# An adaLN transformer block on one core: a prologue with on-chip block table, uniform folds, split state banks and paired modulation groups

## The chip, the cores and the metric

The kernel runs on one NeuronCore of a Trainium2 chip. The metric is the time of one execution on the device in microseconds. A kernel is run several times and the median is given. One more execution is recorded by the hardware profiler; it has a time of its own, and its span is the time from its first to its last instruction.

The engines are named as the profile names them: PE (TensorE, matrix products, with PEld for its weight loads), DVE (VectorE), ACT (ScalarE), POOL (GpSimd) and SP (SyncE, which here only issues DMAs).

## What is computed

```python
x = A_x                                         # 2048 x 640
mod = (silu(c) @ w_mod).reshape(1, 6, 1, 640)
sa, ca, ga, sb, cb, gb = (mod[:, i] for i in range(6))
h = layernorm(x) * (1 + ca) + sa
q, k, v = split(h @ wqkv)                       # 32 heads of 20
pq, pk = q @ w_phi, k @ w_phi                   # per head, 20 x 20
phi = lambda p: concat(softmax(p), softmax(-p))
kv = phi(pk)^T v;  z = sum over s of phi(pk)    # per head
o = (phi(pq) kv) / (phi(pq) z + 1e-6)
x = x + ga * (o @ wo)
h = layernorm(x) * (1 + cb) + sb
out = x + gb * (relu(h @ w1 + b1)^2 @ w2 + b2)  # inner width 1728
```

All data are 32-bit floats. Large products are made of three products of a high and a low part of each operand (`three`, line 84).

## The kernel before

The 2048 tokens are 16 tiles of 128. The work has a **prologue** (lines 146 to 638), a **planned part** in which a planner orders the instructions of the token tiles 2 to 13 (lines 650 to 687), and later parts for the output projection and the two MLP products, whose order is again written out by hand. This case is about the prologue; there the order on every engine is that of the program, once `manual_schedule` is entered (line 196).

The prologue loads weights, folds `w_phi` into the weights of Q and K, computes the scale and shift of the first layer norm for 640 features as columns, and runs the projections of the tiles 0 and 1.

- **Loads.** SP's queue issues them in this order (lines 198 to 232): `c`, the block table `bd`, K's weights (`wk1`, the last 40 columns, then five blocks of 128 rows), x's tokens 0 to 255 (`load_x(0)`), Q's weights in the same way, modulation blocks 0 and 1 (`load_wm`), x's tokens 256 to 511, modulation blocks 2 to 4, V's weights.
- **Block table.** `bd_t` has 128 rows and 640 columns: for a group of six heads a block of 120 x 120, with each head's 20 x 20 matrix on its diagonal, five such groups, and two heads in the last 40 columns. The host fills it, with zeros around the diagonal, and the kernel loads it whole (lines 199 and 200).
- **Warm-up.** `WARM` = 14 products of a tile of ones (line 563) keep PE working until the first weights are there.
- **Folds.** `fold(nm, d)` (line 246) makes 128 rows of a folded weight from six products, five with 120 rows of contraction and one with 40 (`GR`, line 26). Each goes to two banks of PSUM from the pool `pj`, which has four banks. The function that it returns, `split`, copies them to SBUF as a high part (ACT) and subtracts it for the low part (DVE).
- **State.** `kvp` (line 143) is one PSUM tile of three banks. From the first key tile on it collects phi(K)^T V in banks 0 and 1; before that its halves (`half`, `TR`) hold the transposes of the normalised tokens (`t_in`) and the columns of the modulation.
- **Modulation.** For each of five groups of 128 features `mod_rows2(d)` multiplies silu(c) with the block `WM[d]` (10 products), `mod_sb(d)` copies the result to SBUF on ACT, `mod_cols2(d)` transposes it and adds up on DVE; `out0(d)` then applies it to the transposed tokens (ACT twice, DVE once), and `k_step(d)` adds this group's share to the K product of both tiles.
- **Layer norm.** `stats` runs on DVE, with four small operations on POOL; `scale` applies the result on ACT, for 256 tokens at a time.

The order of the last steps (lines 564 to 601): folds k0 to k2, `stats` of x's first block, folds k3 and k4, its `scale`, folds q0 and q1, transposes 0 and 1, fold q2, modulation rows 0, fold q3, columns 0, fold q4, modulation rows 1, transposes 2 to 4, then for each d: columns and `out0` of group d + 1, rows of group d + 2, `k_step(d)`; `stats` of x's second block after step 1 and its `scale` after step 2. After that PK is copied out, and the products Q and V of the tiles 0 and 1 follow (lines 610 to 637).

Of the kernel before, what the change touches and what calls it, by code (L numbers as in the profile page):

```python
# [15 lines left out]
P = 128  # L16
# [18 lines left out]
WARM = 14  # L35
# [16 lines left out]
def kernel(  # L52
# [90 lines left out]
    kvp = psK.tile([P, 3, 512], F32, name="kvp")  # L143


    ones = const.tile([P, P], F32, name="ones")
    nc.gpsimd.memset(ones, 1.0)
    ident = const.tile([P, P], F32, name="ident")
# [45 lines left out]
    ET_ = mybir.EngineType  # L194
    first = tc.manual_schedule(engines={ET_.PE, ET_.DVE, ET_.Activation, ET_.Pool, ET_.SP})
    first.__enter__()

    nc.sync.dma_start(c_t, c)
    bd_t = row("s4", "bd_t")
    nc.sync.dma_start(bd_t, bd)  # L200
    raw, WM, RV, XB = {}, {}, {}, {}

    def load_raw(nm, w5, w1):
        raw[nm] = [tok2("w", f"raw_{nm}{i}") for i in range(3)]
        nc.sync.dma_start(raw[nm][2][:40, 1], w1)
        for d in range(NC):
            nc.sync.dma_start(raw[nm][d // 2][:, d % 2], w5[d * P : (d + 1) * P])

# [14 lines left out]
    for d in range(2):  # L223
        load_wm(d)
    load_x(1)
    for d in range(2, NC):
        load_wm(d)
    for d in range(NC):
        if d % 2 == 0:
            both = tok2("w", f"rawv{d}")  # L230
        RV[d] = both[:, d % 2]
        nc.sync.dma_start(RV[d], wv[d * P : (d + 1) * P])

# [12 lines left out]
    def fold(nm, d):  # L246
# [3 lines left out]
        p = pj(f"fold{nm}{d}")  # L250
        for g, (o, n) in enumerate(GR):
            if g < 5:
                r = raw[nm][d // 2][:n, d % 2, g * P : (g + 1) * P]
            else:
                r = raw[nm][2][:n, 1, d * P : (d + 1) * P]
            nc.tensor.matmul(
                p[g // 3][:, (g % 3) * 120 : (g % 3) * 120 + n], r, bd_t[:n, g * 120 : g * 120 + n],
# [158 lines left out]
    def do_kv(t):  # L416
        v, e = vt[t % 2], EK[t]
        for u, (o, n) in enumerate(UN):
# [3 lines left out]
                kvp[64 * c : 64 * c + 64, g // 4, a : a + 2 * n].rearrange("p (s n) -> p s n", s=2),  # L422
# [92 lines left out]
    def half(b, h):  # L515
        return kvp[:, b, 256 * h : 256 * h + 256]
# [3 lines left out]
    def mod_rows2(d):  # L520

        MR[d] = tp(f"mrow{d}")
        for k in range(NC):
            for s in range(2):
                c = 2 * (k % 2) + s
                a = 256 * k + P * s
                nc.tensor.matmul(
                    MR[d][32 * c : 32 * c + 32, :P], cs[:, k : k + 1].to_broadcast([P, 32]), WM[d][:, a : a + P],
                    start=(k < 2), stop=(k >= NC - 2), skip_group_check=True,
                )  # L530

    def mod_sb(d):
        t = MR[d, "sb"] = row("s1", f"msb{d}")[:, :P]
        nc.scalar.activation(t, MR[d][:, :P], AF.Identity, bias=plus[:, 0:1])

    def mod_cols2(d):
        p = half(0, 1)[:, P * (d % 2) : P * (d % 2) + P]
        nc.tensor.transpose(p, MR[d, "sb"], ident)
        nc.vector.tensor_reduce(
            cols_a.rearrange("p (s d) -> p s d", s=2)[:, :, d],  # L540
            p.rearrange("p (h s r) -> p s h r", h=2, s=2)[:, :, :, 0], axis=AX.X, op=ALU.add,
        )
# [21 lines left out]
    for d in range(3):  # L564
        fold("k", d)()
    n0 = stats(XB[0], "a0")
    for d in range(3, NC):
        fold("k", d)()
    scale(XB[0], *n0)
    for d in range(2):  # L570
        fold("q", d)()
    t_in(XB[0], 0, TR[0])
    t_in(XB[0], 1, TR[1])
    fold("q", 2)()
    mod_rows2(0)
# [989 lines left out]
```

## Time and profile before

| | us |
|---|---|
| median of 3 runs | 801.46 |
| lowest and highest run | 798.03, 801.79 |
| profiled execution | 800.36 |
| its span | 798.7 |
| PE busy in the span | 785.4 |
| PE busy from 7 to 27 us | 19.81 of 20 |
| first fold's first weight load | 6.19 |
| DMA engines busy from 7 to 27 us | 1.02 of 1 |

Times in the trace count from the span's start. Line numbers with an L are those of this kernel. A product in 32 bits shows as two records of PE (14 warm-up products, 28 records). A busy PE is not PE at its peak, since products are pipelined and their ends are modelled. The row of an engine or of DMA activity is busy time, not waiting time; idle time stands in brackets behind a row with what ended it. "PEclk" is the granted clock of TensorE, 1.00 at full speed.

### The profile page before, as it was taken

The numbers are of one execution on the slowest core, as the hardware profiler recorded it, in microseconds if no ns is written. First come the engines' busy times: TensorE is split into PE (matmuls) and PEld (weight loads), VectorE is DVE, ScalarE is ACT, GpSimd is POOL, SyncE is SP. The second block draws the span as 40 slices with busy tenths as digits, with TensorE's granted clock in tenths as the row PEclk, the third lists the DMA queues.
The fourth block names the chain that finished last, engine by engine and source line by source line (L and its number), as shares of the span: only waits on it lengthen the run. The fifth ranks groups of instructions, "written<-read, shape, count | busy, mean of one in ns | idle before, by whom it ended". The sixth has DMA issues, their size and how long they took to land.

```text
span 798.7 us, 15281 instructions
## 1 busy us (share of the span) xinstructions
PE 785.4 (98%) x5983; PEld 750.5 (94%) x5983; DVE 579.3 (73%) x1046; ACT 443.3 (56%) x988; POOL 128.3 (16%) x259
## 2 busy tenths in 40 slices
PE   9999999999999999999999999998999999999997
PEld 8899999999999878898899999998999999999997
DVE  4499889998788688993546666775757667675756
ACT  4667675576753355565777737555364645536431
POOL 3001021010000114331000000131131313213110
PEclk9999999999999999999999999999999999999999
DMA  9713326423120243321347355996575967667450
GB/s 341 279 35 128 115 83 203 148 85 116 67 100 1 82 167 132 116 83 67 116 144 239 130 180 213 284 317 207 160 237 154 278 170 234 200 175 218 122 168 34
DMA packets 50560, 126.30 MB, mean 158 GB/s; under 512 B 5872, under 2 KB 6640, under 8 KB 50488
## 3 DMA queue, kind: packets, MB, share of 16 engines
q1 hardware_dynamic: 33432, 84.32, 31.0%
q0 software_dynamic: 14752, 35.76, 16.3%
q10 hardware_dynamic: 2304, 5.24, 1.7%
q8 instruction: 47, 0.77, 0.4%
q14 instruction: 25, 0.20, 0.1%
HBM read 95.32 MB, written 29.88 MB: 157 GB/s over the span
## 4 chain that ended last, share of the span: by engine, by line
PE 75%; DVE 10%; ACT 6%; issue 4%; POOL 3%; DMA 2%; POOLq 0%; ACTq 0%; DVEq 0%
PE up L78 18%; PE acc L78 14%; PE pk L78 8%; PE pq L78 7%; PE pv L78 7%; PE pwo L78 7%; PE acc3x L78 4%; PE kvp L421 2%; DVE dn L790 2%; DVE scr L788 2%; PE te L829 2%; DMA ring_b<-td_b 1%; PE ta L340 1%; PE tb L340 1%; DVE ezb L809 1%
## 5 line engine op out<-in xcount | busy, mean ns | idle before, releaser
L78 PE MATMUL up<-h,w 128*128 128x256 f32 x1640 | 208.7, 279 | 0.4 <-ACT ft L1149 0.4
L78 PEld LDWEIGHTS up<-h,w 128*128 128x128 f32 x1640 | 197.9, 189 | 1.1 <-ACT ft L1149 0.8
L1149 ACT ACTIVATE ft<-up,b_t 128x256 f32<-128x256 f32 x104 | 49.0, 472 | 106.6 <-PE up L78 106.1
L78 PE MATMUL acc<-w,ra 128*128 128x384 f32 x452 | 100.4, 338 | 0.4
L78 PE MATMUL pwo<-wo,ot 128*128 128x256 f32 (+3 forms) x512 | 83.2, 315 | 0.1
L1150 DVE TENSOR_TENSOR ft<-ft 128x256 f32<-128x256 f32 x104 | 44.0, 423 | 50.5 <-ACT ft L1149 48.8
L78 PE MATMUL pk<-wk,hT 128*128 128x384 f32 (+1 forms) x480 | 77.1, 312 | 0.9 <-ACT hT L352 0.9
L78 PEld LDWEIGHTS pwo<-wo,ot 128*128 128x128 f32 (+1 forms) x512 | 75.7, 188 | 1.9 <-ACT ot L866 0.4
L78 PEld LDWEIGHTS acc<-w,ra 128*128 128x128 f32 x452 | 72.7, 188 | 3.7 <-DVE ra L88 2.0
L78 PE MATMUL pq<-wq,hT 128*128 128x384 f32 (+1 forms) x480 | 74.9, 311 | 0.4 <-ACT k L397 0.4
L78 PE MATMUL pv<-wv,hT 128*128 128x384 f32 (+1 forms) x480 | 75.2, 309 | 0.0
L78 PEld LDWEIGHTS pk<-wk,hT 128*128 128x128 f32 x480 | 71.6, 188 | 2.7 <-ACT hT L352 1.1
L78 PEld LDWEIGHTS pq<-wq,hT 128*128 128x128 f32 x480 | 70.5, 188 | 1.5 <-ACT k L397 0.9
L78 PEld LDWEIGHTS pv<-wv,hT 128*128 128x128 f32 x480 | 70.5, 188 | 0.4
L88 DVE TENSOR_TENSOR ra<-ft,ra 128x384 fp32r<-128x384 f32 (+2 forms) x86 | 36.8, 449 | 34.3 <-ACT ra L1173 21.0
L88 DVE TENSOR_TENSOR h<-hfb,h 128x256 fp32r<-128x256 f32 x40 | 17.0, 425 | 46.4 <-ACT h L352 46.3
L1173 ACT ACTIVATE ra<-ft 128x384 fp32r<-128x384 f32 x48 | 25.2, 526 | 32.6 <-DVE ft L1150 25.2
L78 PE MATMUL acc3x<-w,ra 128*128 128x256 f32 x248 | 43.0, 281 | 0.0
L78 PEld LDWEIGHTS acc3x<-w,ra 128*128 128x128 f32 x248 | 39.5, 188 | 1.6 <-DVE y L1314 1.4
L1259 POOL DMA_DIRECT2D ring_a<-td_a x34 | 18.3, 540 | 129.9 <-PE acc L78 103.3
L792 POOL TENSOR_TENSOR dn<-dn,rs_q 128x64 f32<-128x64 f32 x16 | 14.0, 877 | 128.0 <-DVE dn L790 128.0
L1164 DVE TENSOR_TENSOR ft<-ft 128x128 f32<-128x128 f32 x136 | 33.3, 286 | 1.2
(241 smaller groups left out, 1424.5 us busy)
## 6 DMA issues: line engine op xcount, KB each, us to landing
ring_c<-td_c POOLq DMA_DIRECT2D x34, 384.0 KB, 4.6
ring_a<-td_a POOLq DMA_DIRECT2D x34, 384.0 KB, 4.2
ring_b<-td_b POOLq DMA_DIRECT2D x34, 256.0 KB, 4.5
esp<-eq SPq DMA_DIRECT2D x12, 640.0 KB, 3.0
el<-esp SPq DMA_DIRECT2D x12, 640.0 KB, 3.9
rw<-in_w SPq DMA_DIRECT2D x23, 320.0 KB, 3.1
wm<-in_w_mod SPq DMA_DIRECT2D x20, 320.0 KB, 3.8
xb<-in_x SPq DMA_DIRECT2D x8, 640.0 KB, 4.2
```

Source lines behind the costliest of these rows:

```text
L78: nc.tensor.matmul(o, a, b, start=first and i == 0, stop=last and i == len(terms) - 1, skip_group_check=skip,)
L88: (eng or nc.vector).tensor_tensor(out_lo, full, hi.bitcast(F32), op=ALU.subtract)
L340: nc.tensor.transpose(p[:, i * P : (i + 1) * P], xn[:, i, d * P : (d + 1) * P], ident)
L421: nc.tensor.matmul(kvp[64 * c : 64 * c + 64, g // 4, a : a + 2 * n].rearrange("p (s n) -> p s n", s=2), v[:, u], e[:, :, o : o + n], start ...
L788: nc.vector.tensor_tensor(z, flat(ET[t]), flat(zb), op=ALU.mult)
L790: nc.vector.tensor_reduce(dn.rearrange("p s h -> p (s h)"), heads(z), axis=AX.X, op=ALU.add)
L829: nc.tensor.transpose(p[:m, a : a + P], EU[2 * j + i][:, b : b + m], ident)
L1149: nc.scalar.activation(r, p, AF.Relu, bias=b1_t[:, f : f + 1])
L1150: nc.vector.tensor_tensor(r, r, r, op=ALU.mult)
L1164: nc.vector.tensor_tensor(t[:, o], t[:, a], t[:, b], op=op)
L1173: nc.scalar.activation(a[:, 0, :3], t[:, :3], AF.Copy)
L1259: nc.gpsimd.dma_start(RING[j, n, r], TD[n][r].bitcast(F32R))
```

## The change

- The host gives the 32 matrices of `w_phi` as a 120 x 120 array. The kernel loads that into a corner of `bdc` and spreads it with two products on DVE: the array, repeated, times `own`, a pattern of 120 x 6 ones that POOL makes with one memset and two selections.
- This load and that of `c` are issued by ACT instead of SP.
- `manual_schedule` is entered earlier, before the constants, so POOL's constants are made in the program's order.
- The sixth product of each fold reads 120 rows like the others; the added rows of the weights are zeros that DVE sets with two memsets of 128 x 640 before the loads of `wk1` and `wq1`. Those loads stand behind the first block of their weight.
- All five modulation blocks are loaded ahead of x's second block.
- `kvp` becomes three tiles of one bank. The folds q0 and q3 write to banks 1 and 2 instead of `pj`.
- Modulation groups go in pairs: rows 0 and 1 together, then 2, then 3 and 4, each pair in one bank. The step order is new (below): rows 0 and 1 stand behind fold q3, transposes 1 to 4 behind fold q4, and `scale` of x's second block stands after step 3, behind the last `out0`.
- `WARM` is 9.

The diff, cut to its core:

```diff
-WARM = 14
+WARM = 9
...
     psK_s = ExitStack()
     psK = psK_s.enter_context(tc.tile_pool(name="psK", bufs=1, space=PS))
-    kvp = psK.tile([P, 3, 512], F32, name="kvp")
-
+    kvp = [psK.tile([P, 512], F32, name=f"kvp{b}") for b in range(3)]
+
+
+    ET_ = mybir.EngineType
+    first = tc.manual_schedule(engines={ET_.PE, ET_.DVE, ET_.Activation, ET_.Pool, ET_.SP})
+    first.__enter__()
     ones = const.tile([P, P], F32, name="ones")
     nc.gpsimd.memset(ones, 1.0)
+
+    bdc = row("s3", "bdc")
+    own = bdc[:120, P : P + 6]
+    nc.gpsimd.memset(own, 1.0)
+    nc.gpsimd.affine_select(out=own, in_=own, compare_op=ALU.is_ge, fill=0.0, base=0,
+                            pattern=[[-DH, 6]], channel_multiplier=1)
+    nc.gpsimd.affine_select(out=own, in_=own, compare_op=ALU.is_ge, fill=0.0, base=DH - 1,
+                            pattern=[[DH, 6]], channel_multiplier=-1)
     ident = const.tile([P, P], F32, name="ident")
     make_identity(nc, ident)
     neg = const.tile([P, P], F32R, name="neg")
...
     nc.gpsimd.tensor_tensor(mask5, mask5, mtmp[:80, :40], op=ALU.add)
-    ET_ = mybir.EngineType
-    first = tc.manual_schedule(engines={ET_.PE, ET_.DVE, ET_.Activation, ET_.Pool, ET_.SP})
-    first.__enter__()
-
-    nc.sync.dma_start(c_t, c)
+    nc.scalar.dma_start(bdc[:120, :120], bd)
+    nc.scalar.dma_start(c_t, c)
     bd_t = row("s4", "bd_t")
-    nc.sync.dma_start(bd_t, bd)
     raw, WM, RV, XB = {}, {}, {}, {}
     def load_raw(nm, w5, w1):
         raw[nm] = [tok2("w", f"raw_{nm}{i}") for i in range(3)]
-        nc.sync.dma_start(raw[nm][2][:40, 1], w1)
+        nc.vector.memset(raw[nm][2][:, 1], 0.0)
         for d in range(NC):
             nc.sync.dma_start(raw[nm][d // 2][:, d % 2], w5[d * P : (d + 1) * P])
+            if d == 0:
+                nc.sync.dma_start(raw[nm][2][:40, 1], w1)
     def load_x(j):
         XB[j] = tok2(f"x{j % 2}", f"xb{j}")
...
     load_raw("k", wk5, wk1)
     load_x(0)
     load_raw("q", wq5, wq1)
-    for d in range(2):
+    for d in range(NC):
         load_wm(d)
     load_x(1)
-    for d in range(2, NC):
-        load_wm(d)
     for d in range(NC):
         if d % 2 == 0:
             both = tok2("w", f"rawv{d}")
         RV[d] = both[:, d % 2]
         nc.sync.dma_start(RV[d], wv[d * P : (d + 1) * P])
+
+    by_head = bdc[:120, :120].rearrange("p (g f) -> p g f", f=DH)
+    nc.vector.tensor_tensor(
+        bd_t[:120, :600].rearrange("p (g i f) -> p g i f", i=6, f=DH),
+        by_head[:, :5, None, :].to_broadcast([120, 5, 6, DH]),
+        own[:, None, :, None].to_broadcast([120, 5, 6, DH]), op=ALU.mult
+    )
+    nc.vector.tensor_tensor(
+        bd_t[:120, 600:].rearrange("p (i f) -> p i f", f=DH),
+        by_head[:, 5:6, :].to_broadcast([120, 2, DH]), over(own[:, :2]), op=ALU.mult
+    )
     cs = const.tile([P, NC], F32, name="cs")
     ce = const.tile([P, NC], F32, name="ce")
...
     W = {}
-    def fold(nm, d):
+    def fold(nm, d, p=None):
         w = wslot(f"w{nm}{d}")
         W[nm, d] = w
-        p = pj(f"fold{nm}{d}")
+        p = p or pj(f"fold{nm}{d}")
         for g, (o, n) in enumerate(GR):
             if g < 5:
-                r = raw[nm][d // 2][:n, d % 2, g * P : (g + 1) * P]
+                r = raw[nm][d // 2][:120, d % 2, g * P : (g + 1) * P]
             else:
-                r = raw[nm][2][:n, 1, d * P : (d + 1) * P]
+                r = raw[nm][2][:120, 1, d * P : (d + 1) * P]
             nc.tensor.matmul(
-                p[g // 3][:, (g % 3) * 120 : (g % 3) * 120 + n], r, bd_t[:n, g * 120 : g * 120 + n],
+                p[g // 3][:, (g % 3) * 120 : (g % 3) * 120 + n], r, bd_t[:120, g * 120 : g * 120 + n],
                 start=True, stop=True,
             )
...
             g, c = divmod(u, 2)
             a = 120 * (g % 4)
             nc.tensor.matmul(
-                kvp[64 * c : 64 * c + 64, g // 4, a : a + 2 * n].rearrange("p (s n) -> p s n", s=2),
+                kvp[g // 4][64 * c : 64 * c + 64, a : a + 2 * n].rearrange("p (s n) -> p s n", s=2),
                 v[:, u], e[:, :, o : o + n],
                 start=(t == 0 and g % 4 == 0), stop=(t == NT - 1), skip_group_check=True,
             )
...
             nc.scalar.activation(xt[:, i], xt[:, i], AF.Identity, bias=nb[:, i : i + 1], scale=sq[:, i : i + 1])
     def half(b, h):
-        return kvp[:, b, 256 * h : 256 * h + 256]
+        return kvp[b][:, 256 * h : 256 * h + 256]
     MR = {}
-    def mod_rows2(d):
-
-        MR[d] = tp(f"mrow{d}")
-        for k in range(NC):
-            for s in range(2):
-                c = 2 * (k % 2) + s
-                a = 256 * k + P * s
-                nc.tensor.matmul(
-                    MR[d][32 * c : 32 * c + 32, :P], cs[:, k : k + 1].to_broadcast([P, 32]), WM[d][:, a : a + P],
-                    start=(k < 2), stop=(k >= NC - 2), skip_group_check=True,
-                )
-
-    def mod_sb(d):
-        t = MR[d, "sb"] = row("s1", f"msb{d}")[:, :P]
-        nc.scalar.activation(t, MR[d][:, :P], AF.Identity, bias=plus[:, 0:1])
-
-    def mod_cols2(d):
-        p = half(0, 1)[:, P * (d % 2) : P * (d % 2) + P]
-        nc.tensor.transpose(p, MR[d, "sb"], ident)
-        nc.vector.tensor_reduce(
-            cols_a.rearrange("p (s d) -> p s d", s=2)[:, :, d],
-            p.rearrange("p (h s r) -> p s h r", h=2, s=2)[:, :, :, 0], axis=AX.X, op=ALU.add,
-        )
+    def mod_rows2(*ds):
+
+        p = tp(f"mrow{ds[0]}")
+        for m, d in enumerate(ds):
+            MR[d] = p[:, m * P : m * P + P]
+            for k in range(NC):
+                for s in range(2):
+                    c = 2 * (k % 2) + s
+                    a = 256 * k + P * s
+                    nc.tensor.matmul(
+                        MR[d][32 * c : 32 * c + 32], cs[:, k : k + 1].to_broadcast([P, 32]), WM[d][:, a : a + P],
+                        start=(k < 2 and m == 0), stop=(k >= NC - 2), skip_group_check=True,
+                    )
+
+    def mod_sb(*ds):
+        for d in ds:
+            t = MR[d, "sb"] = row("s1", f"msb{d}")[:, :P]
+            nc.scalar.activation(t, MR[d], AF.Identity, bias=plus[:, 0:1])
+
+    def mod_cols2(*ds):
+        for d in ds:
+            p = half(0, 1)[:, P * (d % 2) : P * (d % 2) + P]
+            nc.tensor.transpose(p, MR[d, "sb"], ident)
+            nc.vector.tensor_reduce(
+                cols_a.rearrange("p (s d) -> p s d", s=2)[:, :, d],
+                p.rearrange("p (h s r) -> p s h r", h=2, s=2)[:, :, :, 0], axis=AX.X, op=ALU.add,
+            )
     TR = [half(0, 0), half(1, 0), half(1, 1), half(2, 0), half(2, 1)]
     mem.tile([P, 48], F32, tag="gap", name="gap", bufs=1)
...
     warm = tp("warm")
     for i in range(WARM):
         nc.tensor.matmul(warm[:, :P], ones, ones, start=True, stop=True)
-    for d in range(3):
+    for d in range(4):
         fold("k", d)()
     n0 = stats(XB[0], "a0")
-    for d in range(3, NC):
-        fold("k", d)()
+    fold("k", 4)()
+    fold("q", 0, kvp[1:])()
+    fold("q", 1)()
     scale(XB[0], *n0)
-    for d in range(2):
-        fold("q", d)()
+    fold("q", 2)()
+    split = fold("q", 3, kvp[1:])
+    mod_rows2(0, 1)
     t_in(XB[0], 0, TR[0])
-    t_in(XB[0], 1, TR[1])
-    fold("q", 2)()
-    mod_rows2(0)
-    mod_sb(0)
-    split = fold("q", 3)
-    mod_cols2(0)
     split()
+    mod_sb(0, 1)
     split = fold("q", 4)
+    mod_cols2(0, 1)
     out0(0)
-    mod_rows2(1)
     split()
-    mod_sb(1)
-    for d in range(2, NC):
+    for d in range(1, NC):
         t_in(XB[0], d, TR[d])
+    mod_rows2(2)
+    mod_sb(2)
     load_x(2)
     PP += [pj(f"pk{t}") for t in range(2)]
+    rows_at, cols_at = {1: (3, 4)}, {1: (2,), 2: (3, 4)}
     for d in range(NC):
+        mod_cols2(*cols_at.get(d, ()))
         if d + 1 < NC:
-            mod_cols2(d + 1)
             out0(d + 1)
-        if d + 2 < NC:
-            mod_rows2(d + 2)
+        if d in rows_at:
+            mod_rows2(*rows_at[d])
         k_step(d)
-        if d + 2 < NC:
-            mod_sb(d + 2)
+        mod_sb(*rows_at.get(d, ()))
         if d == 1:
             n1 = stats(XB[1], "a1")
-        if d == 2:
+        if d == 3:
             scale(XB[1], *n1)
     def v_hi(d):
...
-    bd = np.zeros((P, D), A_w_phi.dtype)
+    bd = np.zeros((6, DH, 6, DH), A_w_phi.dtype)
     for h in range(H):
-        i = h % 6
-        bd[i * DH : (i + 1) * DH, h * DH : (h + 1) * DH] = A_w_phi[h]
+        bd[h % 6, :, h // 6] = A_w_phi[h]
...
-        "bd": bd,
+        "bd": bd.reshape(120, 120),
```

More of the change, by code (lines that the diff above doesn't have):

```diff
@@ L712 @@
     kvs = flat(tok2("w", "kvs"))
-    nc.scalar.activation(kvs[:, :480], kvp[:, 0, :480], AF.Copy)
-    nc.scalar.activation(kvs[:, 480:600], kvp[:, 1, :120], AF.Copy)
-    nc.scalar.activation(kvs[:64, 600:680], kvp[:64, 1, 120:200], AF.Copy)
+    nc.scalar.activation(kvs[:, :480], kvp[0][:, :480], AF.Copy)
+    nc.scalar.activation(kvs[:, 480:600], kvp[1][:, :120], AF.Copy)
+    nc.scalar.activation(kvs[:64, 600:680], kvp[1][:64, 120:200], AF.Copy)
     psK_s.close()
```

## The prediction

> **What bounds the kernel now.** First the page's busy times and the table by stage (start and end of a stretch, its length, busy time of PE, its weight loads, DVE, ACT and POOL, granted clock, DMA share, GB/s).
>
> ```profile
> PE 785.4 (98%) x5983; PEld 750.5 (94%) x5983; DVE 579.3 (73%) x1046; ACT 443.3 (56%) x988; POOL 128.3 (16%) x259
> ```
> ```profile
> 7.00:27.00 20.00, 19.81 (x189) 17.13 (x187) 11.49 (x29) 12.10 (x27) 1.40 (x4) 1.00 1.02 413
> ...
> 100.00:200.00 100.00, 99.36 (x769) 96.53 (x766) 94.86 (x130) 63.38 (x144) 11.22 (x16) 1.00 0.39 127
> ```
>
> TensorE (PE) is hardly ever without work, so a gain must take PE work away or remove one of its few waits. The change rewrites the prologue, and there a second resource is full: from 7 to 27 us the DMA engines are busy 1.02 of 1 and move 413 GB/s. So I read PE's order there in the chain of waits, and beside it when the loads land.
>
> ```profile
> 6.19 8.19 PEld L256 LDWEIGHTS foldk<-bd_t,raw_k 120*128 120x128 f32 x60
> ```
> ```profile
> 20.36 0.78 PE mrow L527 x20
> ...
> 24.49 0.78 PE mrow L527 x20
> 25.27 0.81 PE kvp L340 x6
> 26.08 0.11 PE kvp L538
> 26.19 0.78 PE mrow L527 x20
> 26.96 1.95 PE pk L78 x12
> ...
> 30.73 0.81 DVE sta L503 x2
> ...
> 34.70 1.73 ACT xb L513 x2
> ...
> 37.39 2.12 PE pk L78 x12
> 39.51 4.31 PE pq L78 x30
> ```
>
> The folds run from 6.19, the K product starts at 26.96, the Q product at 39.51. From there on PE has the same work in both kernels; what the change brings is how much earlier the 39.51 comes.
>
> SP's queue tells the landings, because each of these issues waits until the load eight places ahead of it has landed.
>
> ```profile
> 0.80 0.39 SPq L198 DMA_DIRECT2D c_t<-in_c  x1
> 1.25 0.42 SPq L200 DMA_DIRECT2D bd_t<-in_bd  x1
> ...
> 4.92 0.75 SPq L205 DMA_DIRECT2D raw_q<-in_wq  x1
> ```
> ```profile
> 12.83 0.36 SPq L215 DMA_DIRECT2D wm<-in_w_ss  x1
> ```
> ```profile
> 15.89 0.33 SPq L232 DMA_DIRECT2D rawv<-in_wv  x1
> ```
> ```profile
> 18.98 0.33 SPq L232 DMA_DIRECT2D rawv<-in_wv  x1
> ```
> ```profile
> 20.50 0.33 SPq L232 DMA_DIRECT2D rawv<-in_wv  x1
> ```
>
> Counting eight back: wq's first block has landed by 12.83, its last by 15.89, the modulation blocks wm0 by 18.98 and wm1 by 20.50. PE uses wm0 at 20.36 and wm1 at 24.49, so these loads come 1.4 and 4.0 us early today.
>
> **The change part by part.**
>
> *Nine warm-up matmuls for fourteen*, two records each:
>
> ```profile
> 1.90:5.30 3.40, 3.40 (x18) 3.40 (x18) 1.00 0.90 251
> 5.30:6.19 0.89, 0.89 (x10) 0.89 (x9) 1.00 0.83 319
> ```
>
> The upper row's 18 records include one cut off at each end: 3.40/16 = 0.21 us each; after 5.3 it is about half. What goes is the fast part. Eighteen slow records take 3.8 us and end at 1.05 + 3.8 = 4.9, so folds can start 1.3 us earlier than 6.19.
>
> Is their data there? The block table now comes by a 56 KB load on ACT's queue and a DVE product. The nearest rows:
>
> ```profile
> c_t<-in_c SPq DMA_DIRECT2D x1, 2.5 KB, 1.8
> ```
> ```profile
> L605 ACT ACTIVATE wv<-rawv 128x640 fp32r<-128x640 f32 x5 | 3.3, 734 | 0.0
> L404 DVE TENSOR_TENSOR ek<-k,mxk 128x640 f32<-128x640 f32 x4 | 3.1, 822 | 0.1
> ...
> L88 DVE TENSOR_TENSOR wk<-foldk,wk 128x360 fp32r<-128x360 f32 x5 | 2.6, 519 | 5.1 <-ACT wk L263 5.1
> ```
>
> The tiny load lands 1.8 us after its issue, so the block lands at 2.6; at worst like the whole table today, by 4.92. The product over 600 columns costs 600/640 of 822 ns = 0.77, its tail 0.2 at most. Table ready: 3.6 to 5.9. I take 4.2, nearer the small load, since the block has a sixth of the table's bytes. DVE's two memsets ahead of it take no more than a pass of two operands over as many columns (0.82 each) and end by 2.4, before the block lands; POOL's pattern of six columns ends well before. At the late end PE waits 1.0 us, which falls into the waits for loads found below.
>
> *Folds on 120 rows.* A fold is ten records with 120 rows and two with 40:
>
> ```profile
> 7.83:8.94 1.11, 1.10 (x10) 1.00 1.03 408
> 8.94:9.48 0.54, 0.39 (x3) 1.00 1.02 408
> ```
>
> Ten weight loads fill 1.11 us; the narrow pair takes 0.54, though it moves a third of the columns, with 0.15 idle. At 120 rows two should take no more than their neighbours, 0.22: 0.32 saved per fold, 1.33 for 1.65 (bounds 0, and 0.43 if narrow columns cost half). The Trainium skill ("TensorEngine Tiling (Array Packing)", Tiling Modes) lists two tiles of 64 rows for short contractions, up to twice as fast, which speaks for the narrow form; its Key Properties add that a change of mode drains the array. By the first the ten folds gain nothing, by the second what the 0.54 row shows, 3.2 us of PE work.
>
> *Loads.* The table shrinks by 264 KB, 0.65 us at 413 GB/s. It and c leave SP's queue, so bulk data is asked for at 0.80 instead of 1.25, 0.45 us; SP's second issue then waits for the first memset, to about 1.5, and the block's own bytes take some back. I take 0.8 us earlier for all that follows (bounds 0.3 and 1.1). x's second block moves behind wm4 and lands near 26; it is first read at 30.73, by the statistics.
>
> *Where PE then stands.* Folds from 4.9, 0.3 for the rest of the slow part, five of K at 1.33: 11.8. wq's first block: 12.83 - 0.8 = 12.0, a wait of 0.2. Four folds of Q: 17.3. DVE's subtractions per fold (0.52 for 360 columns, so 0.92 for 640) and the statistics (2 x 0.81 and two short steps) keep pace, since two of these folds use the state banks and so wait for no buffer. Now comes the pair of modulation rows, which needs wm0 and wm1: 18.98 - 0.8 = 18.2 and 20.50 - 0.8 = 19.7. PE waits 0.9, works 0.78, waits 0.7. **The loads take over as the bound.** Behind wm1 stand: rows of group 1 0.78, two transposes 0.27 (0.81/6 each), the last fold 1.33, two column transposes 0.22, eight transposes 1.08, rows of group 2 0.78: together 4.5, and the K product starts at 24.2 instead of 26.96. **Gain 2.8.** Of the 1.3 + 3.2 us of PE work removed, the rest turns into waiting.
>
> *The last wait before the Q product.* PE stood 0.94 us (its record at 37.39) because ACT ran the second block's scale (1.73) ahead of the last hidden block. The scale now stands behind it. The five steps keep their length, so the last starts near 33.8. Late next would be ACT's eviction of pk: scale from 32.3 to 34.0, one copy of 0.73 to 34.7, and the first eviction is due at 34.8. **Gain 0.9.** Without that cover, up to 0.9 comes back. Pairing groups 3 and 4 moves no work off PE; both have landed by 24.4 and are used from 26.
>
> *Three bank tiles, new order later.* The planned part from 58 us comes out in a new order: the same instructions, some interleaved differently. I take 0, bounds one microsecond either way: PE idles only 0.64 of 100 us there, but DVE at 94.86 leaves little room.
>
> Sum: 2.8 + 0.9 = 3.7 us. The profiled execution took 800.36 us (span 798.7 and 1.7 around it) and would take 796.7. It stands 1.1 below the median of 801.46 (798.03 to 801.79), which becomes **797.8**.
>
> **The rivals.**
>
> *The loads are not late.* Between wq's last block and wm0 lie 3.09 us, between wm0 and wm1 1.52, for 640 KB each: 1.5 us of wm0 are not its bytes. Without that delay wm1 is there at 18.2, PE runs on from 17.3 + 0.78, and the K product starts at 22.7: gain 4.3 + 0.9 = 5.2, 796.3. Against it: nothing in the diff touches the delay. 0.20.
>
> *The clock drops in the new waits.* The trace has one such case:
>
> ```profile
> 541.20 1.01 PE L78 MATMUL acc<-ring_b,rs 128*128 128x256 f32 x3 [2.17 <-DMA ring_b<-td_b]
> ```
> ```profile
> 542.00:544.00 2.00, 2.00 (x11) 0.50 0.78 234
> 544.00:546.00 2.00, 2.00 (x14) 0.85 0.65 202
> ```
>
> A wait of 2.17 us was followed by half clock until 544.6 (0.85 of the second row's 2 us: 0.6 at half), 3.4 us that cost 1.7. Here PE would wait 1.6 of 2.4 us. The cost would lie behind wm1: 799.5. 0.15. The Trainium skill ("TensorE: Matmul & The Clock Gate", The HAM clock gate) halves the clock after a whole idle window of some 3.4 us. By that rule these waits are too short; the row shows that a shorter one sufficed.
>
> *It doesn't do what it says*: the narrow pair keeps its 0.54. PE reaches the modulation rows at 18.8, wm1 still binds, and only the last fold costs 0.3 more: 798.1, inside the forecast. With the new order taking 3 us as well: 801. 0.10.
>
> *Slower: the new order makes PE wait for DVE* in the planned part, some twelve tiles long. If one DVE pass of 0.82 us per tile gets ahead of what PE needs: 9.8 - 3.7 = 6.1 on top, 807.6. It turns from faster to slower at 0.31 per tile. For it: DVE at 94.86 of 100. Against it: PE's sequence of products is nearly unchanged. 0.10.
>
> **How the numbers follow.** Forecast 0.45, own range 796 to 800 (loads 0.3 to 1.1 earlier; the spread of the runs). A measurement of this kernel can tell about 0.5%, 4.0 us, so the forecast lies just inside. Faster by more: 0.18 of the forecast's 0.45, 0.18 of the first rival, 0.03 of the others: 0.39. Slower: 0.08 of the last rival. Same: 0.53. The range of 795.0 to 801.3 leaves out the slower rival and the tails.
>
> **What would show it.** Folds from 4.9 with twelve evenly spaced records; PE waiting near 0.2 before the first fold of Q, 0.9 and 0.7 around the first modulation rows, released by the wm loads; the K product at 24.2, the Q product at 35.8, no wait of 0.94; PE as busy as now from 58 to 340. Wrong if the Q product starts after 37, if the granted clock falls below 1 before 30 us, or if PE's waits from 58 to 340 grow by over 2 us.

## The result, and the profile after

The kernel after takes **791.55 us** (median of 9 runs, 791.15 to 796.52). The kernel before took 798.03 in 9 runs (796.93 to 801.79). The ratio is 0.9931, with a 95% interval of 0.9914 to 0.9947: 6.5 us faster. The forecast of 797.8 with its range of 795.0 to 801.3 lies above that. The profiled execution took 791.25 us (span 789.5); that of the kernel before had 800.36.

Busy times of the page first, then a row of the table by stage (start and end of a stretch, its length, busy time of PE, its weight loads, DVE, ACT and POOL, granted clock, DMA share, GB/s), both of the kernel after:

```profile
PE 778.3 (99%) x5973; PEld 746.5 (95%) x5973; DVE 582.0 (74%) x1050; ACT 441.4 (56%) x988; POOL 128.6 (16%) x262
```
```profile
7.00:27.00 20.00, 19.65 (x236) 18.52 (x236) 12.48 (x33) 13.27 (x31) 2.11 (x8) 1.00 1.03 406
```

PE is as busy as before in the prologue (19.65 of 20 us for 19.81), and DMA is still full. The 236 records for 189 show mainly that PE is further along: the stretch holds 40 more records of modulation rows and 13 more of the K product, beside 109 of folds for 116.

The chain of waits of the kernel after (start, length, engine, tile, line, number of records) shows the new prologue:

```profile
1.05 4.21 PE warm L586 x18
5.26 7.13 PE foldk L275 x60
12.38 1.34 PE kvp L275 x12
13.72 2.68 PE foldq L275 x24
16.41 1.34 PE kvp L275 x12
17.75 1.44 PE mrow L548 x40
...
20.81 0.15 PE kvp L561
20.96 0.02 issue
20.99 0.17 DVE cols_a L562
21.16 0.14 issue
21.30 0.30 PE kvp L561
...
23.25 1.93 PE pk L78 x12
...
34.68 4.31 PE pq L78 x30
```

The K product starts at 23.25 (26.96 before, 24.2 forecast) and the Q product at 34.68 (39.51 before, 35.8 forecast). That is 4.83 us gained, 3.71 ahead of the K product and 1.12 behind it; forecast were 2.8 and 0.9. PE meets no wait for a load. A new one lies at 20.96: a column transpose stands still until DVE has read the one before it. The table of PE's waits of the kernel after (total, times, longest) sums it up:

```profile
PE kvp L561 <- DVE cols_a L562: 0.7, 2, 0.4
```

SP's queue tells the landings of wm0 and wm1, by the issues eight places behind them. The kernel after first, then a second execution of the kernel before (run b_again below):

```profile
16.58 0.33 SPq L240 DMA_DIRECT2D rawv<-in_wv  x1
```
```profile
18.12 0.33 SPq L240 DMA_DIRECT2D rawv<-in_wv  x1
```
```profile
17.57 0.33 SPq L232 DMA_DIRECT2D rawv<-in_wv  x1
```
```profile
19.12 0.33 SPq L232 DMA_DIRECT2D rawv<-in_wv  x1
```

The forecast used 18.98 and 20.50 from the first execution of the kernel before. In the second one the same loads landed 1.4 us earlier, and from there to the kernel after they moved by 1.0 us (forecast 0.8). The 1.5 us that were "not its bytes" do not stay with wm0. The same issues tell these landings in all 19 profiled executions, and most stand 1.5 to 1.6 us apart. A step of over 2 us lies ahead of wm0 in the first execution before (3.09) and in b_scale3 (3.08), ahead of wm1 in b_k120 (2.28), a_k40 (2.79), a_fullbd (2.67), a_w5 (3.03) and a_best (2.14), and ahead of wm2, where PE does not wait, in the kernel after (2.21, to 20.33) and in a_cols (2.10). Which block this tail meets was chance, as far as these executions show.

PE's busy time from 58 to 340 us after, and in the 282 us that answer to it before:

```profile
58.00:340.00 282.00, 280.05 (x2113) 1.00 0.32 109
```
```profile
63.00:345.00 282.00, 280.11 (x2113) 1.00 0.33 109
```

The same records in the same time: the planned part's new order costs nothing, as forecast. The lead at the first MLP product (404 us) is 4.92 against the first execution before, 5.09 against the second.

A last piece lies at 541 us, where the kernel before waits for `ring_b`. In each pair: the row of PE's waits, then PE busy, clock and DMA from 541 to 552; the first execution before, then the second.

```profile
PE acc L78 <- DMA ring_b<-td_b: 2.2, 1, 2.2
```
```profile
541.00:552.00 11.00, 10.80 (x74) 0.84 0.59 174
```
```profile
PE acc L78 <- DMA ring_b<-td_b: 1.3, 1, 1.3
```
```profile
541.00:552.00 11.00, 10.52 (x79) 1.00 0.61 168
```

In the second execution the wait ends at 539.20, and the 15 records behind it take 1.93 us; in the first they take 3.10. The wait of 2.2 us and the half clock behind it, which the prediction quoted for its clock rival, belong to that execution: in the 18 others the longest wait for `ring_b` is 0.3 to 1.7 us. Other executions of either kernel may be longer in this way: of those with their clock on record, the longest (before 800.69 and 800.72, after 795.96 and 796.52) have a mean granted clock of 0.994 to 0.997, most others 0.998 or more. The first execution is 0.6 us behind the second at 475 us, 1.1 ahead of the wait and 3.5 at 552.

### The profile page after: what moved, and what is told of

Its sections match the earlier page's. It is cut to its first block, busy times and chain, and to the rows that moved or that the text cites. A ratio compares the mean times of both kernels' runs of the same rounds, so it can differ in the third digit from the quotient of the medians.

```text
span 789.5 us, 15269 instructions
## 1 busy us (share of the span) xinstructions
PE 778.3 (99%) x5973; PEld 746.5 (95%) x5973; DVE 582.0 (74%) x1050; ACT 441.4 (56%) x988; POOL 128.6 (16%) x262
## 4 chain that ended last, share of the span: by engine, by line
PE 84%; DVE 8%; ACT 3%; issue 2%; POOL 1%; DMA 1%; POOLq 0%; ACTq 0%; DVEq 0%
PE up L78 21%; PE acc L78 16%; PE pk L78 9%; PE pq L78 8%; PE pv L78 8%; PE pwo L78 7%; PE acc3x L78 5%; PE kvp L440 3%; DVE dn L811 2%; DVE scr L809 2%; PE te L850 2%; PE tb L359 1%; DMA ring_b<-td_b 1%; PE foldk L275 1%; DVE ezb L830 1%
## 5 line engine op out<-in xcount | busy, mean ns | idle before, releaser
L468 DVE TENSOR_REDUCE rs_q<-eq 128x64 f32<-128x1280 f32 x16 | 23.5, 1475 | 15.0 <-ACT eq L427 15.0
```

What stands on the lines that cost most here:

```text
L468: nc.vector.tensor_reduce(s, heads(flat(e)), axis=AX.X, op=ALU.add)
```

## The experiments

Theory 1: the gain is PE work removed and waits removed, the terms add up, and loads bind (the forecast) or do not (its first rival). Theory 2, formed after the first runs: the parts cover for each other, so one part alone is worth little. "Q" is the first weight load of the Q product: 39.24 before (39.12 in b_again), 34.40 after. Runs given with one time are single; before took 796.93 beside the first four, 797.25 beside the next four, 797.43 and 797.88 beside the rest (medians). Q comes from one execution of each kernel, and it moves by some 0.4 us with the moment at which PE reaches full pace (a_bdfirst).

### b_again: the kernel before, unchanged

> The kernel before, unchanged, profiled once more. The yardstick for all looks at the prologue is the first weight load of the Q product: 39.24 us in the first profile of before, 34.40 in that of after. If the prologue is set by its own order, it comes out at 39.2 again, within the phase of the clock's release (0.5 us). For the rest: the profiles of before and after differ by 9.1 us, of which 3.2 lie at one wait of 2.17 us for ring_b near 541 us with the half clock behind it. If that wait belongs to the kernel before, it is here again and the execution takes about 800; if it is chance, it is gone and the execution takes about 797.

796.50, Q 39.12; rows above. The prologue repeats within 0.12 us, the landings and the wait at 541 do not.

### b_k120: before, all folds on 120 rows

```diff
-        nc.sync.dma_start(raw[nm][2][:40, 1], w1)
+        nc.vector.memset(raw[nm][2][:, 1], 0.0)
...
+            if d == 0:
+                nc.sync.dma_start(raw[nm][2][:40, 1], w1)
...
-                r = raw[nm][2][:n, 1, d * P : (d + 1) * P]
+                r = raw[nm][2][:120, 1, d * P : (d + 1) * P]
```

> Before, with the folds on 120 rows alone (zero rows set by DVE, wk1 and wq1 behind their first block). If PE's own work sets the prologue, each of ten folds is 0.31 shorter and the Q product's first weight load comes 3.1 us earlier, at 36.1. If the loads bind, PE reaches the first modulation rows at 17.8 and waits for wm0 to 19.0: gain 1.9, 37.3. If the narrow pair is no slower than it must be, nothing changes: 39.2.

797.04, Q 38.90. Of 3.2 us of PE work, 0.3 arrive. PE's waits in its prologue:

```profile
PE foldq L258 <- DVE wk L88: 1.1, 1, 1.1
...
PE foldk L258 <- DMA raw_k<-in_wk: 0.8, 1, 0.8
PE foldq L258 <- DVE wq L88: 0.4, 1, 0.4
```

The faster folds run into a full `pj` (2 waits on DVE, 1.5 us) and into K's weights (0.8). The chain of this run shows what stands behind the full `pj`:

```profile
4.46 7.88 DMA xb<-in_x
12.37 0.90 DVE sta L505 x2
...
16.26 1.73 ACT xb L515 x2
...
18.97 1.53 PE foldq L258 x12
```

x's first block lands at 12.34; its statistics and its scale follow, and only then are the folds of Q evicted. Faster folds cannot pass that. In the kernel after, the scale stands behind two folds of Q; that step was not tested alone. This is the first sign of theory 2.

### b_w9: before, nine warm-ups

```diff
-WARM = 14
+WARM = 9
```

> Before, with 9 warm-up products for 14. The first weight block lands at 5.54, so folds can start there instead of 6.19: 0.6 us, Q product at 38.6. In before the loads wm0 and wm1 end 3.2 us after their first part has landed. If that tail comes from PE's instruction fetch, which takes a DMA engine for 0.95 us at 16.3, twenty fewer PE instructions move the fetch and the tail with it; if the tail comes from the order or the shape of the loads, wm0 lands near 19.0 and wm1 near 20.5 as before.

808.70, Q 51.09: **11.9 us later**. The chain row of its K folds, then its stretch from 10 to 20 us (columns as in the stage table), then PE alone in that stretch of the kernel before:

```profile
5.88 15.01 PE foldk L256 x60
```
```profile
10.00:20.00 10.00, 10.00 (x43) 9.13 (x41) 4.77 (x13) 3.09 (x7) 1.40 (x4) 1.00 1.03 417
```
```profile
10.00:20.00 10.00, 9.81 (x73) 1.00 1.03 416
```

Five folds take 15.01 us, 3.0 each for 1.65. The profile shows PE as busy throughout, at 43 records in 10 us for 73. The PEclk column reads 1.00 in both rows, so half pace does not show there; I read the clock from the pace of the records.

The expectation also asked for the tail of the loads. Here each landing behind wq's last block follows the one before by 1.5 to 1.6 us. The one packet of the kind "instruction" among these DMA transfers comes between 22.5 and 23 us; it comes as late in b_w9r, and between 23 and 23.5 in a_w5k40, also without a tail. In 14 of the 15 executions that have that packet between 14.5 and 17.5 us, one of the three landings behind wq's last block is 1.7 to 3.1 us behind the one before. The exception is b_again, with the packet between 16 and 16.5 and no such step. So the fetch of instructions is the likeliest source of the tail, but this is not shown.

### b_scale3: before, x's second scale behind step 3

```diff
-        if d == 2:
+        if d == 3:
             scale(XB[1], *n1)
```

> Before, with the scale of x's second block moved behind the last out0 and nothing else. If the wait of 0.94 us goes and nothing is late behind it, the Q product's first weight load comes at 38.3. If ACT's copies of pk are then late, because the scale (1.73) stands right before them, 0.3 to 0.9 of it comes back: 38.6 to 39.2.

798.24, Q 39.10: 0.14 earlier than before. Two rows of PE's waits:

```profile
PE foldk L256 <- DMA raw_k<-in_wk: 0.6, 1, 0.6
PE pq L78 <- ACT k L397: 0.5, 1, 0.5
```

The first is a late load of K's weights, which belongs to this execution: the K product starts at 27.44, 0.48 later than before. From there to Q it is 11.66 us for 12.28 before, so the edit itself is worth some 0.6 of the 0.94 us. The rest moved to the Q product, which now needs a PSUM bank that ACT is late to evict: the "late next" that the forecast named and put at zero.

### a_k40: after, the sixth product on 40 rows

```diff
-                r = raw[nm][2][:120, 1, d * P : (d + 1) * P]
+                r = raw[nm][2][:n, 1, d * P : (d + 1) * P]
...
-bd_t[:120, g * 120 : g * 120 + n],
+bd_t[: (120 if g < 5 else n), g * 120 : g * 120 + n],
```

> After, with the sixth product of each fold on 40 rows again. If PE's own work sets the prologue, ten times 0.31 come back and the Q product's first weight load moves from 34.40 to 37.5. If the loads bind, as forecast, PE only waits less: 35 at most.

793.88, Q 36.93, 2.53 later. The edit that was worth 0.3 alone is worth 2.5 among the others.

### a_w14: after, fourteen warm-ups

```diff
-WARM = 9
+WARM = 14
```

> After, with 14 warm-up products. Ten more records at 0.11: folds start at 6.1 to 6.2 instead of 5.14. If PE's own work sets the prologue, the Q product moves by 1.0 to 35.4; if the loads bind behind it, it stays at 34.4 to 34.7.

792.58, Q 34.91, 0.51 later. The five warm-ups, forecast at 1.3, are worth 0.5.

### a_x1first: after, x's second block ahead of the modulation blocks

```diff
+    load_x(1)
     for d in range(NC):
         load_wm(d)
-    load_x(1)
```

> After, with x's second block loaded ahead of the modulation blocks, so that these come 1.5 us later: wm0 near 18.1 and wm1 near 19.7. That is the case the forecast had assumed. PE should wait some 0.4 before the first modulation rows and 0.8 before the second, the Q product at 35.6. If the modulation blocks have slack, it stays at 34.4.

794.67, Q 36.04, 1.64 later. The row of PE's waits that appears:

```profile
PE mrow L548 <- DMA wm<-in_w_ss: 1.5, 2, 0.9
```

Here the loads bind, in waits of 0.6 and 0.9 ahead of the two groups of rows, where the forecast had 0.9 and 0.7: its mechanism exists, once the blocks land later than they do in the kernel after.

### a_pj: after, the folds q0 and q3 in the pool's banks

```diff
-    fold("q", 0, kvp[1:])()
+    fold("q", 0)()
...
-    split = fold("q", 3, kvp[1:])
+    split = fold("q", 3)
```

> After, with folds q0 and q3 in the pool's four banks instead of the state banks. DVE is held by the statistics (11.9 to 14.0) and subtracts fold k4 only from 13.9; a fold two places on must wait for that. If the state banks buy time, PE waits 1 to 2 us between folds q0 and q3 and the Q product comes at 35.5 to 36.5; if DVE would have kept pace anyway, 34.4.

793.23, Q 35.47, 1.07 later, with one new wait of PE:

```profile
PE foldq L275 <- DVE wk L88: 0.7, 1, 0.7
```

This is a wait in which b_k120 lost a part of its gain; the two further banks remove it.

### a_fullbd: after, the host's table loaded whole by SP

```diff
-    nc.scalar.dma_start(bdc[:120, :120], bd)
...
+    nc.sync.dma_start(bd_t, bd)
...
-    nc.vector.tensor_tensor(
-        bd_t[:120, :600].rearrange("p (g i f) -> p g i f", i=6, f=DH),
...
```

> The kernel after, with the block table filled by the host and loaded whole, by SP ahead of K's weights, as in the kernel before; nothing is spread on the chip, c stays on ACT's queue. This undoes the first part of the change alone. Theory A (loads have slack in the kernel after, since wm1 landed at 18.1 and PE reached the modulation rows at 17.7 with no wait): the bulk loads move 0.6 to 0.8 us later, wm0 to about 17.3 and wm1 to 18.8; the rows of group 0 start at 17.7, those of group 1 at 18.1, so PE waits at most 0.7; the first fold starts near 5.1, as now; the Q product starts at 34.4 to 35.1. Theory B (the forecast's: the loads bind): the Q product is later by the whole of the table's 0.65 us and more, 35.1 to 35.6. If the table lands later than the 4.2 of now, the folds start by as much later.

792.69, Q 35.44, 1.03 later. PE's one wait for a load:

```profile
PE mrow L530 <- DMA wm<-in_w_ss: 0.9, 1, 0.9
```

The size lies in Theory B's range, and the wait is larger than Theory A allowed. But the larger load need not be the cause: wm0 lands at 16.63, for 16.58 in the kernel after, and only wm1 is late, at 19.30 behind a step of 2.67. That is the tail, which a_k40 and a_w5 show with the small table. So what the small table is worth stays open. The blocks have little slack in the kernel after: wm1 lands at 18.12 and its rows are due at 17.75 + 0.72 = 18.47.

### a_onekvp: after, the state as one tile

```diff
-    kvp = [psK.tile([P, 512], F32, name=f"kvp{b}") for b in range(3)]
+    kvp_ = psK.tile([P, 3, 512], F32, name="kvp")
+    kvp = [kvp_[:, b] for b in range(3)]
```

> The kernel after, with the state again as one tile of three banks; the folds q0 and q3 still use banks 1 and 2 of it. Theory A: waits between engines go by tiles, so the folds' evictions, the transposes and the column steps of different banks wait for each other: PE waits for ACT's or DVE's evictions of q3 before the first transposes and for the reductions, the Q product starts 1 to 2 us later than 34.40. Theory B: waits go by the addresses that an instruction touches, and the split into three tiles changes nothing: Q product at 34.4, with no new wait in its prologue. In the planned part both expect the same order or one that costs less than 1 us.

793.75, Q 36.59, 2.19 later. PE's waits that are new:

```profile
PE kvp L562 <- ACT msb L557: 0.9, 1, 0.9
PE kvp L360 <- ACT hfa L371: 0.9, 1, 0.9
```

Theory A holds. The first transposes, the evictions of fold q3 and `out0` touch different banks, but in one tile they queue behind one another. The forecast had no term for this.

### a_bdfirst: after, the small table's load on SP ahead of K's weights

```diff
-    nc.scalar.dma_start(bdc[:120, :120], bd)
+    nc.sync.dma_start(bdc[:120, :120], bd)
```

> The kernel after, with the small table's load issued by SP ahead of K's weights instead of by ACT. In the kernel after it is issued by ACT at 0.80 and lands at 4.21, 3.4 us later; the product on DVE starts then (4.30) and the folds at 5.14. Theory A: the landing is late because the first bulk load, asked for at about the same time, fills the queues of the DMA engines; put ahead of it, the table lands earlier, by 3.0 to 3.5, and the first fold starts at the end of the warm-up, near 4.9 to 5.0, 0.2 us earlier at most; the bulk loads are later by 0.3 to 0.5. Theory B: 120 rows of 480 bytes take that long wherever they stand; the table lands at 3.8 to 4.4, the folds start within 0.3 us of 5.14. Q product 34.2 to 34.7 by both, so the second queue is worth half a microsecond at most.

791.47, Q 34.03. DVE's product on the table (duration; first and last start), after and in this run:

```profile
L243 DVE TENSOR_TENSOR bd_t<-bdc x1: 784/784/784, 4.3 to 4.3; 120x600 f32<-120x600 f32 x1
```
```profile
L243 DVE TENSOR_TENSOR bd_t<-bdc x1: 782/782/782, 2.8 to 2.8; 120x600 f32<-120x600 f32 x1
```

The table is there 1.5 us earlier than on the second queue, where it ran beside the first bulk load; what held it there is not shown. But the folds begin at 5.26 in both, behind the warm-ups, so the load was not late for them. The 0.37 us come from an earlier full pace in this execution: the five K folds take 6.73 us for 7.13.

### a_cols: after, both column transposes ahead of both reductions

```diff
         for d in ds:
-            p = half(0, 1)[:, P * (d % 2) : P * (d % 2) + P]
-            nc.tensor.transpose(p, MR[d, "sb"], ident)
+            m = P * (d % 2)
+            nc.tensor.transpose(p[:, m : m + P], MR[d, "sb"], ident)
+        for d in ds:
```

> The kernel after, with the column step of a pair rewritten: both transposes first, then both reductions. In the kernel after PE waits 0.7 us before the second transpose of a pair (2 waits, the longest 0.4), released by DVE's reduction of the first. Theory A: the second transpose waits because the first half of the same tile is being read; with both transposes ahead of both reductions that wait is gone, the Q product starts 0.7 us earlier than 34.40, at 33.7, and the end is as much earlier, about 790.9 against 791.6. Theory B: PE only waits elsewhere, because the hidden block out0 that DVE and ACT make from these columns is what is late; the 0.7 us reappears ahead of the first K product or of a later step, the Q product stays at 34.2 to 34.4, and the time stays within 0.3 us. In both, the times of single runs still scatter by 1 to 5 us.

791.28 (median of 6), ratio to before 0.9915 (0.9894 to 0.9937), Q 33.39, 1.01 earlier. The chain rows of the two column pairs:

```profile
20.88 0.24 PE kvp L562 x2
...
28.26 0.22 PE kvp L562 x2
```

Two transposes in 0.24 us, with DVE no longer between them. Theory A holds in the trace. In the time, 0.3 us below the kernel after, the interval is too wide to show it.

### b_w9r, b_w9k120: nine warm-ups before, again, and with uniform folds

> The kernel before with nine warm-ups for fourteen, once more. The first look at it gave 808.70 and a Q product at 51.09, 11.85 us late, with PE at half speed until 34 us. Theory A (half speed follows from what PE does between 1 and 34 us: the wait of 0.6 us behind the warm-ups and the narrow records of the folds): it comes again, Q product after 45, time over 804. Theory B (chance of when the clock's interval begins in an execution): this time the clock is released before 10 us, the Q product is at 38 to 40, the time 796 to 798.

809.30, Q 51.26: it was not chance.

> The kernel before with nine warm-ups and with the sixth product of each fold on 120 rows, both together; the wait for K's weights behind the warm-ups stays. Theory A (the narrow records with their idle time hold the clock back): it is released within 7 us of the folds' start, Q product at 38 to 39.5, time 796 to 798. Theory B (the wait behind the warm-ups does it): half speed until after 15 us again, Q product after 45. Theory C (chance): as A, and then the second look at nine warm-ups alone is early as well.

795.44, Q 38.60. The timeline of its fold weight loads (idle time and its releaser in brackets):

```profile
5.22 1.51 PEld L258 LDWEIGHTS foldk<-bd_t,raw_k 120*128 120x128 f32 x12 [0.26 <-issue]
8.03 5.43 PEld L258 LDWEIGHTS foldk<-bd_t,raw_k 120*128 120x128 f32 x48 [1.30 <-DMA raw_k<-in_wk]
```

Full pace from the first fold on (12 loads in 1.51 us), through a wait of 1.30. But K's loads stand in another order here, so the wait lies behind the first fold; a_w5 and a_w5k40 remove that difference.

### a_w5, a_w5k40: after, five warm-ups, with folds on 120 rows and on 40

```diff
-WARM = 9
+WARM = 5
```

a_w5k40 has the edit of a_k40 as well.

> The kernel after with five warm-ups for nine. Their ten records end at 3.3 and the block table is ready at 5.0, so PE waits 1.7 us ahead of the folds. Theory A (a wait behind the warm-ups keeps the clock at half): the folds run at 0.22 us for each record instead of 0.11, Q product after 45, time 800 to 805. Theory B (uniform folds are enough to release the clock): released by 9 us, Q product at 34.4 to 36.5, time 791 to 793.5, with a wider scatter than with nine.

> The kernel a_w5 (the kernel after with five warm-ups) with the sixth product of each fold on 40 rows again, nothing else. In a_w5 PE records came at 6 in 1 us until 9.0 and at 10 to 12 in 1 us from then on, with the Q product at 35.92. Theory A (the narrow records hold the clock at half, once it has not been released before the folds): 4 to 5 records in 1 us through all ten folds, full speed only during the modulation rows or later, Q product after 44, time over 800. Theory B (the clock is released after some microseconds of folds of either kind, and the kernel before had another cause): full speed by 13 us, Q product at 38 to 40.5, time 794 to 797.

a_w5: 792.82 (median of 4), ratio to before 0.9941 (0.992 to 0.9963), Q 35.92. a_w5k40: 807.57, Q 50.75. The K folds in the chain and PE by stretches, a_w5 and then a_w5k40:

```profile
5.09 8.81 PE foldk L275 x60
```
```profile
8.00:9.00 1.00, 1.00 (x6) 1.00 0.99 343
9.00:10.00 1.00, 1.00 (x10) 1.00 1.05 407
```
```profile
4.98 15.04 PE foldk L275 x60
...
31.99 2.70 PE mrow L548 x40
...
35.31 1.72 PE foldq L275 x12
```
```profile
10.00:20.00 10.00, 10.00 (x42) 1.00 1.03 418
20.00:30.00 10.00, 10.00 (x42) 1.00 0.78 307
```

Both wait about 1.5 us for the table ahead of the folds. On 120 rows the pace doubles at 9 us, 4 us into the folds. On 40 rows it stays at 42 records in 10 us, with PE never idle, for the 27 us of folds from 4.98 to 31.99. Forty modulation rows still take 2.70 (1.44 after); the last fold, at 35.31, is at full pace. The rows of one product in six make the difference of 14.8 us. In a_k40 the same narrow folds took only 8.30 us for five: there nine warm-ups had brought full pace by 5.5 us. So they held back a full pace that had not yet come, and did not end one that had. The Trainium skill ("TensorE: Matmul & The Clock Gate", The HAM clock gate) releases the clock after one busy window of some 3.4 us. a_w5 agrees; a_w5k40 and b_w9 do not, with 27 us and more of a PE that the profile shows as busy. The Trainium skill ("TensorEngine Tiling (Array Packing)", Tiling Modes) says that a change of tiling mode drains the array; if the gate counts drained time as idle, that would explain it, but no run here measured the drain by itself.

### a_best: a_cols and a_bdfirst together

> The kernel after with both small edits: the column step with both transposes ahead of both reductions (alone: Q product 1.01 us earlier, ratio to before 0.9915), and the small table's load on SP ahead of K's weights (alone: 0.37 us earlier). Theory A (the second gain is the clock's chance, since the folds start at the same time with it): Q product at 33.2 to 33.6, time 790 to 791.3, as with the column step alone. Theory B (they add up): Q product at 33.0, time 0.4 us below the column step alone. Theory C: PE, now earlier, waits for the modulation loads at 17.3, 0.2 to 1 us, and the second gain is lost.

791.19 (median of 5), ratio to before 0.9911 (0.9897 to 0.9925), Q 34.00. One wait of PE is back:

```profile
PE mrow L548 <- DMA wm<-in_w_ss: 0.9, 1, 0.9
```

Theory C, in part by chance: the second group of rows is due at 17.27 + 0.78 = 18.05, and wm1 lands at 18.95 here, behind the tail, for 18.36 in a_cols. Its time is that of a_cols; beside the kernel after, its lead of 0.4 us lies within the intervals.

## Why the prediction was wrong

It missed by 6.25 us. 3.43 of them are **the anchor**: the median of 801.46, from three runs, two of them above 801, against 798.03 from nine. The step "the profiled execution stands 1.1 below the median" took both for typical. The profile itself held a wait of 2.2 us at 541 with half clock, which no other profile shows. The other 2.82 are **the gain**, 6.48 for 3.66: 1.1 in the prologue, where the loads had been put down as the bound, and 1.7 behind the Q product, most of it not traced.

- **Nine warm-ups, folds from 4.9.** They start at 5.14 to 5.26: right. The value of 1.3 was mis-sized: fourteen cost 0.51 (a_w14), since the folds then start 0.95 later but the five of K take 6.63 us for 7.13. The risk was missing: with the old folds the same edit costs 11.9 (b_w9, b_w9r).
- **The table at 4.2 plus 0.8.** DVE's product starts at 4.3 and takes 0.784: right. The two memsets, put at no more than 0.82 each, took 0.592:

```profile
L213 DVE MEMSET raw_k<- 128x640 f32 x1 | 0.6, 592 | 1.0 <-PEq L1574 1.0
```

- **A fold of 1.33.** The rows show 1.34. The mechanism is right; the worth of 2.53 (a_k40) is near the 3.2. The 0.54 row, a pair of records that lasts longer than its work, was the best evidence in the profile.
- **"The loads take over as the bound."** This step failed. wm1 landed at 18.12, not 19.7, and PE lost none of the 1.8 us put down for loads. The fault was the base: 20.50 came from one execution, with the tail ahead of wm0, and 19.12 stood in the next. "Nothing in the diff touches the delay" was beside the point, since the delay does not stay with one block; in the profiled execution after it lies behind wm1. The rival *loads are not late* had the right picture for that execution, with some luck in where the tail fell: K product at 22.7, measured 23.25. The difference is folds that end 0.6 later than forecast (12.38 for 11.8) and a column wait of 0.4. a_x1first, with its blocks loaded later, and a_fullbd and a_best, with the tail ahead of wm1, show how near the bound is: they wait 0.9 to 1.5.
- **The clock in the new waits.** That rival's condition did not arise, since PE had no such waits. In a_x1first, which has waits of 0.6 and 0.9, the fold behind them takes 1.43 us, as in the kernel after: full pace.
- **Not foreseen: the column wait**, 0.7 us in two places, shown by a_cols. The prediction moved a pair of transposes into one bank without asking who reads it in between.
- **The last wait, 0.9.** Measured 1.12 behind the K product. Right within the whole change; alone it brings some 0.6 (b_scale3).
- **Planned part 0.** Right: 280.05 busy for 280.11. The slower rival did not occur.

The sum to the Q product is 4.83 for 3.7. From there to 404 us the lead is 4.9 to 5.1, and 5.25 between the profiled execution after and b_again. Why the medians differ by 1.2 us more than that was not traced; b_again's 796.50 is one execution of a kernel whose medians here lie at 797.43 to 798.03. The waits for the MLP's two rings differ from execution to execution (together 2.8 and 1.5 before, 1.2 after) and are the likeliest place.

**Theory 2 stands for the prologue.** Alone, uniform folds bring 0.3, the later scale some 0.6, nine warm-ups cost 11.9; together with banks and load order they bring 4.8. Taken back one at a time from the kernel after, five parts (a_k40, a_w14, a_x1first, a_pj, a_onekvp) cost 7.9 in sum. Each part removes the wait into which another's gain would turn: banks the wait for evictions, the order of the loads that for wm, uniform folds the risk of half pace. The pairs of modulation groups, the new step order and the place of the first scale were not taken back alone.

## What to carry to other kernels

Take a second profile of the kernel before, or bound a landing by its spread, before a load that lands "late" carries a forecast: here one tail of 1.5 us decided between two cases. Where several resources are close to each other, cost a change as a whole with its next wait, and not as a sum of single edits. Count records per microsecond, not busy time, when TensorE's first microseconds matter.

## What the runs showed of the hardware

- One narrow product in six (40 rows among 120) kept TensorE at half pace for 27 us, although the profile shows PE as busy throughout: 42 records in 10 us (a_w5k40), against full pace 4 us into uniform folds (a_w5). The granted clock's column showed 1.00 meanwhile. Where full pace came by 5.5 us, the same products did not take it away (a_k40).
- A wait of 2.17 us at 541 was followed by half clock until 544.6 (before); waits of 1.74 (a_w14) and 1.29 us (b_again) for the same ring were not.
- The landing of the same load differed by 1.4 us between two executions of one kernel (wm0 18.98 and 17.57). A step of 1.7 to 3.1 us between landings that otherwise stand 1.5 to 1.6 apart came in 14 of 15 executions with an instruction packet between 14.5 and 17.5 us, at one block or another.
- A 56 KB load issued at 0.8 on the second queue let DVE start at 4.3; on SP's queue ahead of the bulk loads, at 2.8. A queue of its own did not make it land as early.
